# Seven block products for eight in the second feed-forward stage, with a new table of order

## The chip, the cores and the metric

The kernel runs on one core of a Trainium2 chip. Six queues matter here: TensorE (PE in the profile, PEld for its weight loads), VectorE (DVE), ScalarE (ACT), GpSimd (POOL), SyncE (SP, which issues most DMAs), and ScalarE's own DMA queue. The metric is device time in microseconds (us) of one execution; lower is better.

## The reference

Inputs are fp32. Attention over 2 batches, 8 heads, 768 positions and 64 dimensions is masked by equal hash buckets; two feed-forward stages follow it, on 1536 tokens of width 512:

```python
q_bits = (np.einsum('bhsd,dk->bhsk', q, proj) > 0)      # k likewise; proj is 64 x 6
mask = q_bucket[:, :, :, None] == k_bucket[:, :, None, :]
scores = np.where(mask, scale * q @ k.T, -1e9)
x = softmax(scores) @ v                                 # -> (1536, 512)
h = x @ w_in                                            # (512, 2048)
g = np.where(h >= 1, h, np.where(h <= -1, 0.0, (h + 1) ** 2 / 4))
y = g @ w_out                                           # first stage
return ((y @ w_a) * (y @ w_b)) @ w_out2                 # second stage, d_ff = 1536
```

The weights reach the device as 64-bit words, so each tile of them is rebuilt on chip from two 32-bit halves.

## The kernel before, in words

Every fp32 matrix product is done in three terms: an operand is split into a high part (a copy rounded to fp32r) and a low part (the operand less the high part), and high by high, high by low and low by high are added in PSUM. So each operand costs a copy (ScalarE or VectorE) and a subtraction (GpSimd or VectorE) besides the matmuls.

Tokens are worked in `NBLK` = 4 blocks of `TB` = 384. In the first stage (`kind` "in" and "out", `F1` = 16 slices) hidden slices of 128 are made from the 4 chunks of the width, and are added into 4 accumulators. In the second stage (`F2` = 12 slices) a slice f of block blk takes one contraction "a" and one "b" (`contract`, 12 matmuls each: 4 chunks x 3 terms, 384 columns), `t = a * b` (one copy out of PSUM, one product), a split of t into gh and gl, and "out2": 3 token tiles x 3 terms of 512 columns into `acc0` to `acc2`. Attention of the second batch runs beside the first blocks of the first stage.

The second stage's weights are made once: `conv_one` fetches a tile (`stage`, SP), joins its halves (one ScalarE and two VectorE instructions, into `wab`), and `keep` splits it into `wkh` and `wkl`, which stay in SBUF for all four blocks.

The order of the work on every engine is written out: `ORDER` is a table of 2,961 entries, and each entry names an engine and the next operation, as a step from the one before. Dependencies add the semaphores. Buffers come from pools with a set number of slots: `G` takes the space that attention leaves, `F` is the large one, `p` are two PSUM banks, `s0` one, `acc` four.

In PSUM and SBUF the names are `ap` and `bp` (contractions of the second stage), `hp` (of the first), `acc` (outputs), `xsh`/`xsl` (split activations), `y` (output of the first stage), `tk`, `tq`, `kp`, `kid`, `s` (attention's tiles), `plo` and `ptl` (low part of the probabilities, and its transpose by DMA).

At the start the projections `prj` come by two DMAs on SP, and six plus two dummy matmuls (`keep_busy`, tile `idle`) stand in a fixed place between attention's first transposes and its first `kp`.

Of the kernel before, what the change touches and what calls it, by code (L numbers as in the profile page):

```python
# [9 lines left out]
F32 = mybir.dt.float32  # L10
# [24 lines left out]
s s2 a4 v v-6 p10 v v p-5 s20 a-19 s23 s-28 v p11 p p a v-9 p10 s-17 v42 g a-17 v4 a-12 p3 a p-3 a s7 v p-5 a s7  # L35
v v p s-23 v p32 a v-10 a210 g v-200 v-7 p8 a p-12 v p19 p-4 s233 a v-237 a8 p2 s-1 a24 g a-45 v15 a s-4 v p33
s219 v-248 g9 a-4 a5 g13 v7 v p-20 v p-6 s335 a-324 p-2 a p-3 a v-7 a p24 v s-9 v208 v-198 p8 a a25 g a-43 p-6 v
a v211 g-193 a g8 p-12 v p6 a p v p7 v s-20 a s-11 a14 p19 a v-7 p4 a v-72 s285 p-197 v p-4 a-22 a19 p-4 v8 v4
v-11 v8 p6 v a170 v p-164 g-100 p67 s35 s-38 g16 a205 v g-253 g62 a6 a-22 v19 a31 a-35 v-62 v233 s-175 a s-26
p38 a p p26 v v v-27 s-9 s-1 g12 a p3 a p-14 a17 p-2 a v7 v-48 p36 a p23 a v s-13 g7 p14 v s-8 a-30 a18 g-49 g-1  # L40
a95 g p-52 v a s3 v-7 p9 v v160 p-141 v-4 a g8 p-12 a8 p11 a-20 v2 s188 p-180 v a10 a209 g s-217 p20 v-54 a55 v
p a v p-22 a-14 v13 p6 a p27 v p-33 v a-7 a179 p-138 a-22 v-1 v162 v s-141 a27 g p-53 v p14 v a11 s-14 a p40 a v
a-54 g16 v123 v-144 p38 s-47 p34 a14 g5 a-24 p20 a v-17 g10 a g-33 s138 g-92 v-47 p35 v p-6 v p28 a v s-40 p48 a
s141 p-167 v a187 v-267 s57 p49 v32 v a-72 v18 a90 v p-77 a8 a-26 a22 p19 v v-23 p54 a s-58 a p-12 v v s-5 p41 a
g-23 g9 s-27 p36 v s39 p-52 v a-8 s11 p28 a v36 p92 p-126 v v v-3 a-28 a-4 g22 a g16 p-20 v p-15 p31 v v44 g a55
v a-122 a144 v a-140 v21 p9 a v66 p-56 p-2 v a-23 a19 v82 g-121 g52 s-67 p40 p15 v g-3 p-3 p35 a-25 v-9 v57 a21
p-61 v18 s107 a v-125 s-32 g34 a-19 v22 v121 a-125 a14 p-4 v s-43 p37 v p15 a v-15 p16 v p7 a-19 g27 p15 s-52
v53 s-15 a-8 p p28 v-117 s59 g10 v113 a-85 v s14 s-29 p3 a-1 v7 g-10 s2 a-3 v12 s13 g-1 a13 p10 v-38 a70 a-69
g70 v-32 p-27 v a p41 v a-38 g18 a g6 p-10 v-71 p57 v-10 v25 a a11 v11 p-17 v p17 a p13 v a-31 a34 a-2 v-14 s-43
p30 v v p28 v p-17 a v p32 v s16 g-37 s-31 a69 a8 p-42 a v21 v13 v8 v-7 v-17 p-34 a a v s71 a g-88 g-25 v42 v72  # L50
a-59 p2 a a s-40 p57 a v-34 p41 a-4 g v-25 v59 a-44 a23 p-16 v s269 v-288 a g p23 p-2 v10 s-20 p17 v s66 a v
p-41 v-18 v60 a-41 s-45 a18 a11 p3 s23 a-22 v29 p-15 a p-25 v g10 v a-5 v p23 s-8 s-19 a-2 a38 p-55 v83 g-20 v21
p-50 a p21 v a-16 p10 v s-32 v8 p16 a4 a5 a13 g22 v-39 v-7 v8 p19 a a a-4 p-7 v a s34 v-24 p7 v p-35 p-2 p57 a32
s-68 s57 v-92 p66 a2 s-112 a116 v-33 p17 a5 v-1 v44 p22 a s-91 s104 p-67 a v-17 a p6 v5 g9 a-34 p19 v7 p-5 p31 v
a-4 p-18 v a-119 v137 a-10 v a-4 g-19 s-33 v72 p-15 g-41 p65 a61 a-94 v25 g18 s-41 a8 a p-6 a v12 v-6 a18 p-9 v
a-69 p111 a v-34 v-18 v p39 a-30 s13 v10 p25 v p-32 v a-4 v s-35 p31 a17 v18 g-17 p25 v-38 a15 a v p-21 a7 a28
# [24 lines left out]
a64 g p-74 v p6 v a-6 p32 v p-30 p14 a v-14 a27 g-23 g-42 p59 v v30 g p-38 g18 p4 a-14 v-7 a18 g12 v-69 p53 a8 a
s-13 v5 a p40 p-3 p-19 a v-11 a a-6 g p7 v a p28 v p-3 p-14 v s486 v-485 p11 p-16 v p7 v p36 a-50 a17 v-10 v-67
# [162 lines left out]
def attn_moe_kernel(ctx: ExitStack, tc: tile.TileContext, q, k, v, proj,  # L245
                    w_in, w_out, w_a, w_b, w_out2, consts, codes, out):
    nc = tc.nc
# [13 lines left out]
    WARM = 8  # L261
    NB1, NB2 = 6, 2
    RW = 3
    RL = 3
    AGAIN = "out", 5
    KEEP = 2
    NK = 27
# [945 lines left out]
```

## Time and profile before

| | |
|---|---|
| three runs before | 812.21 us median (811.88 to 812.91) |
| the profiled execution | 814.48 us, of which 812.6 us is the span from the first to the last instruction |
| PE busy | 783.4 us |
| DVE, ACT, POOL busy | 539.0, 414.1, 279.1 us |

How to read the profile: busy time of TensorE counts a matmul until its modelled end, so that consecutive matmuls overlap; the distance from one start to the next is what a matmul costs. For the other engines the time from one start to the next in a dense stretch is likewise a little less than the duration that a row gives.

### The profile page before, as it was taken

How to read it: one execution, taken by the hardware profiler on the slowest of the kernel's cores; microseconds unless marked ns; L12 is line 12 of the kernel's file. 1: busy time of each engine (PE TensorE's matmuls, PEld its weight loads, DVE VectorE, ACT ScalarE, POOL GpSimd, SP SyncE). 2: the span in 40 equal slices, each digit the busy share in tenths (PEclk: the TensorE clock that was granted, in tenths of full speed). 3: DMA queues.
4: the chain of work that ended last, by engine and by line, in shares of the span. 5: the costliest groups of instructions: out<-in, count | busy, mean ns of one | idle time of the engine just before them, and what ended most of it. 6: DMA issues, size and time to landing. Idle time of an engine off the chain costs nothing.

```text
span 812.6 us, 14548 instructions
## 1 busy us (share of the span) xinstructions
PE 783.4 (96%) x5716; PEld 728.2 (90%) x5716; DVE 539.0 (66%) x953; ACT 414.1 (51%) x732; POOL 279.1 (34%) x228
## 2 busy tenths in 40 slices
PE   7898799899999999999999999999999999999997
PEld 4677699899888999999999999999999999999997
DVE  5999799999998897989788788644322142133111
ACT  5998699798886876866454565312210111011101
POOL 1767444527564757652332310302100010011101
PEclk9999999999999999999999999999999999999999
DMA  6999999999978877750203454521010010001001
GB/s 187 201 220 206 207 230 261 217 175 248 219 131 166 171 139 133 120 110 1 78 29 107 150 156 129 156 78 52 4 37 1 0 40 1 1 1 40 0 1 40
DMA packets 197509, 90.28 MB, mean 111 GB/s; under 512 B 165056, under 2 KB 191936, under 8 KB 197440
## 3 DMA queue, kind: packets, MB, share of 16 engines
q1 hardware_dynamic: 197152, 89.15, 49.9%
q8 instruction: 45, 0.74, 0.4%
q10 hardware_dynamic: 288, 0.20, 0.1%
q14 instruction: 24, 0.20, 0.1%
HBM read 48.44 MB, written 3.15 MB: 63 GB/s over the span
## 4 chain that ended last, share of the span: by engine, by line
PE 79%; DVE 10%; DMA 5%; issue 2%; ACT 2%; POOL 1%; SPq 0%; DVEq 0%; POOLq 0%; ACTq 0%
PE hp L1021 14%; PE acc L1069 14%; PE ap L1021 12%; PE bp L1021 12%; PE acc L1105 12%; PE s L637 5%; PE pv L709 4%; DMA ptl<-plo 3%; DVE mn L640 2%; PE kp L541 1%; DVE plo L358 1%; DVE wlo L358 1%; PE kid L559 1%; DVE F L926 1%; PE tk L469 1%
## 5 line engine op out<-in xcount | busy, mean ns | idle before, releaser
L358 POOL TENSOR_TENSOR plo<-sm,phi 128x768 f16<-128x768 f32 x66 | 114.6, 1745 | 71.7 <-DVE phi L355 23.0
L358 POOL TENSOR_TENSOR gl<-t,gh 128x384 fp32r<-128x384 f32 x41 | 42.8, 1044 | 255.3 <-ACT gh L353 165.6
L1089 DVE TENSOR_TENSOR t<-t,bp 128x384 f32<-128x384 f32 x48 | 26.6, 553 | 121.6 <-PE bp L1021 121.6
L642 ACT ACTIVATE sm<-s,mn 128x768 f32<-128x768 f32 x96 | 86.2, 898 | 31.9 <-DVE mn L640 27.3
L640 DVE TENSOR_REDUCE mn<-s 128x1 f32<-128x768 f32 x96 | 91.2, 951 | 11.8 <-PE s L637 11.0
L353 ACT ACTIVATE gh<-t 128x384 fp32r<-128x384 f32 x62 | 32.4, 523 | 110.5 <-DVE t L1089 62.2
L353 ACT ACTIVATE t<-ap 128x384 f32<-128x384 f32 x27 | 13.2, 490 | 119.8 <-PE ap L1021 116.5
L1021 PE MATMUL ap<-xsh,wkl 128*128 128x384 f32 x192 | 64.5, 336 | 0.0
L358 POOL TENSOR_TENSOR wlo<-F,whi 128x512 fp32r<-128x512 f32 x35 | 48.9, 1403 | 45.2 <-ACT whi L353 19.3
L1021 PE MATMUL ap<-xsl,wkh 128*128 128x384 f32 x192 | 64.4, 336 | 0.0
L1021 PE MATMUL bp<-xsl,wkh 128*128 128x384 f32 x192 | 64.3, 335 | 0.0
L1021 PE MATMUL ap<-xsh,wkh 128*128 128x384 f32 x192 | 64.3, 335 | 0.0
L1021 PE MATMUL bp<-xsh,wkl 128*128 128x384 f32 x192 | 64.3, 335 | 0.0
L1021 PE MATMUL bp<-xsh,wkh 128*128 128x384 f32 x192 | 64.2, 334 | 0.0
L920 ACT ACTIVATE wab<-stage 128x512 f32<-128x512 f32 x71 | 47.1, 664 | 32.2 <-DVE wkl L358 8.9
L353 ACT ACTIVATE phi<-sm 128x768 f16<-128x768 f32 x71 | 59.2, 840 | 1.0
L637 PE MATMUL s<-kh,qt 128*128 128x384 f32 x192 | 55.4, 370 | 2.5 <-ACT sm L642 2.4
L1105 PE MATMUL acc<-wkh,gl 128*128 128x512 f32 x144 | 56.9, 395 | 0.0
L1105 PE MATMUL acc<-wkl,gh 128*128 128x512 f32 x144 | 56.7, 394 | 0.0
L1105 PE MATMUL acc<-wkh,gh 128*128 128x512 f32 x144 | 56.0, 389 | 0.0
L1043 ACT ACTIVATE t<-hp,half 128x384 f32<-128x384 f32 x64 | 36.8, 575 | 35.2 <-PE hp L1021 34.4
L1021 PE MATMUL hp<-xsh,whi 128*128 128x384 f32 x152 | 52.1, 343 | 0.1
(170 smaller groups left out, 2238.7 us busy)
## 6 DMA issues: line engine op xcount, KB each, us to landing
stage<-in_moe_w_out SPq DMA_DIRECT2D x31, 512.0 KB, 4.2
stage<-in_moe_w_in SPq DMA_DIRECT2D x16, 512.0 KB, 4.4
stage<-in_moe_w_a SPq DMA_DIRECT2D x12, 512.0 KB, 3.7
stage<-in_moe_w_b SPq DMA_DIRECT2D x12, 512.0 KB, 3.7
kn<-in_k SPq DMA_DIRECT2D x16, 192.0 KB, 3.8
out<-ob SPq DMA_DIRECT2D x12, 256.0 KB, 2.0
vn<-in_v SPq DMA_DIRECT2D x4, 384.0 KB, 4.8
vscan<-in_v SPq DMA_DIRECT2D x4, 384.0 KB, 5.0
```

What stands on the lines that cost most here:

```text
L353: nc.scalar.activation(dst, src, ACTF.Copy)
L358: (nc.vector if e == "dve" else nc.gpsimd).tensor_tensor(dst, a, b, ALU.subtract)
L637: nc.tensor.matmul(s()[:, i, 0:HC], x()[:, qs], t[i]()[:, 0:HC], start=(n == 0), stop=(n == 1))
L640: add({"dve": c_dve(S)}, lambda e: nc.vector.tensor_reduce(mn(), s()[:, :, 0:HC], AX.XY, ALU.min), r=[s], w=[mn])
L642: o = add({"act": c_act(S, True) + 0.093}, lambda e: nc.scalar.activation(sm().rearrange("p (c n) -> p c n", c=2), s()[:, :, 0:HC], ACTF.E ...
L709: nc.tensor.matmul(o[:, t, 0:D + 1 - i], w()[:, t, c, :], vcs[t]()[:, c, (1 - i) * D:(2 - i) * D + 1 - i], start=(n == 0), stop=(n == 3 * ...
L920: add({"act": 0.556}, lambda e: nc.scalar.activation(ab(), t()[:, :, :, 1].bitcast(F32), ACTF.Prelu, scale=SHIFT, alpha=SIGN), r=[t], w=[a ...
L1021: nc.tensor.matmul(o()[:, 0:TB], a()[:, kk, :], m(), start=(n == 0), stop=(n == 3 * KD - 1))
L1043: add({"act": 0.465}, lambda e: nc.scalar.activation(t(), o()[:, 0:TB], ACTF.Relu, bias=half, scale=0.5), r=[o], w=[t])
L1069: nc.tensor.matmul(ac()[:, 0:TB], a()[:, d, :], x(), start=(f == 0 and n == 0), stop=(f == F1 - 1 and n == 2))
L1089: add({"dve": c_dve(TB)}, lambda e: nc.vector.tensor_tensor(t(), t(), o()[:, 0:TB], ALU.mult), r=[o], w=[t])
L1105: nc.tensor.matmul(ac(), a()[:, ts], x().rearrange("p k n -> p (k n)"), start=(f == 0 and n == 0), stop=(f == F2 - 1 and n == 2))
```

## The change

The second stage takes two token blocks together. With a1, a2 and b1, b2 the two halves (over the width) of the a- and b-weights of a slice, and the activations of two blocks in halves b11, b21 (first block) and b12, b22 (second), the eight half-contractions are replaced by seven, on sums and differences of weights (s1 to s4) and of activations (t1 to t4). A half-contraction (`product`) is 2 chunks x 3 terms = 6 matmuls of 384 columns. Three PSUM banks X (`mx`), Y (`acc3`) and Z (`mz`) collect them, and `ca`, `cb`, `cc` in SBUF hold what is combined.

- `main` of the second stage: two passes sb, each with 12 slices "ab" and "ab2", the out2 of the first block between them, and then the 12 out2 of the second block from the kept products `cc`.
- Weights: hi and lo parts aren't kept any more. For each slice and pass `weights` forms four sums (128 x 256, tile `ws`), splits three pairs of 512 columns (`wkh`, `wkl`) and one of 256 (`wkb`). The joined words stay in `G` for the first `KA` = 7 slices; those of the other 5 are fetched and joined again for the second pass. `osplit` splits w_out2 for each block anew.
- Activations: `tsplit` forms eight differences (`td`) and ten splits (`tph`, `tpl`) beside the usual split of one block, at the end of the first stage and again during the out2 of block 1.
- The projections' two DMAs go on ScalarE's queue; the dummy matmuls are ordered only before the first score tile; GpSimd may take the high part of the probabilities; and the whole table `ORDER` is another one (3,520 entries), for attention and the first stage too.

```diff
-zb = Buf("z", None, None)
+zb, zz = Buf("z", None, None), Buf("z", None, None, "zz")
 def projections():
-        add({"sp": DMA["tiny"]}, get, w=[(zb, 0)])
...
+        for i in range(2):
+            nc.scalar.dma_start(out=prj[i * D:(i + 1) * D], in_=proj)
...
-        add({"act": c_act(S), "dve": c_dve(S, True)}, lambda e: copy_on(e, hi()[:, jj, :], sm()),
+        add({"act": c_act(S), "dve": c_dve(S, True), "pool": 0.1 + S * 1.55e-3}, ...
...
-    for blk in range(NBLK):
-        ab = [[("a", blk, f), ("b", blk, f)] for f in range(F2)]
-        main += ab[0]
+    n1 = len(main)
+    for sb in range(NBLK // 2):
         for f in range(F2):
-            if f + 1 < F2:
-                main += ab[f + 1]
-            main.append(("out2", blk, f))
+            main.append(("ab", sb, f))
+            if f:
+                main.append(("out2", 2 * sb, f - 1))
+            main.append(("ab2", sb, f))
+        main.append(("out2", 2 * sb, F2 - 1))
+        main += [("out2", 2 * sb + 1, f) for f in range(F2)]
...
+    lasts[max(i for i in range(n1) if main[i][0] == "in")] = "ab", 0
+    lasts[main.index(("out2", 1, F2 // 4))] = "ab", 1
...
+    def pair(src, view, hi, lo, n):
+        add({"act": c_act(n), "dve": c_dve(n, True)}, lambda e: copy_on(e, hi(), view()), r=src, w=[hi.buf])
+        add({"pool": c_pool(n), "dve": c_dve(n)}, lambda e: sub_on(e, lo(), view(), hi()), ...)
...
+    def weights(sb, f):
+        wa, wb = (w32[f, k] if f < KA else w32.pop((f, k)) for k in "ab")
...
+        # s1 = b1 + b2, s3 = a1 - b1, s2 = s1 - a1, s4 = a2 - s2
+            add({"pool": c_pool(h), "dve": c_dve(h)}, lambda e, ...: add_on(e, d(), x(), y(), op), ...)
...
+    def ab(i, sb, f):
+        mop[i] = product(X, X, u[0], 0, "b11", p, True, [s1])
+        product(Y, Y, u[0], 1, "b21", p, True)
+        snap(s1, X, X)
+        plus(s1, Y, Y, ALU.add)
+        product(X, X, u[2], 1, "t2", p, False, [s2])
+        product(Z, zv, u[2], 0, "t1", p, True)
+        snap(s2, X, X)
+        product(X, X, u[3], 0, "t3", p, False, [s3])
+        snap(s3, X, X)
+        plus(s3, Z, zv, ALU.add)
+
+    def ab2(sb, f):
+        product(X, X, u[1], 0, "t4", p, False)
+        product(Z, zv, u[3], 1, "b22", p, False)
+        plus(s1, X, X, ALU.mult)
+        gt[2 * sb, f] = split(s1)
+        plus(s2, Z, zv, ALU.add)
+        add({"pool": c_pool(TB), "dve": c_dve(TB)}, ... s3 = s3 * s2 ...)
+        gt[2 * sb + 1, f] = s3
```

On TensorE at the very start of the program, before: six key transposes (`tk`), then dummy matmuls, then the query transposes (`tq`), more dummies, and the first hash product `kp`.

```order
L469 MATMUL tk<-cst,kn 128x128 x6
L454 LDWEIGHTS warm
L454 MATMUL idle<-warm 128x512
...
L509 MATMUL tq<-eye,qsh 128x128 x3
...
L541 MATMUL kp<-qt,zq_h 103x384
```

The same place after the change:

```order
L529 MATMUL tq<-eye,qsh 128x128 x3
L489 MATMUL tk<-cst,kn 128x128 x6
L474 LDWEIGHTS warm
L474 MATMUL idle<-warm 128x512
...
L562 MATMUL kp<-qt,zq_h 103x384
L562 MATMUL kp<-qt,zq_l 103x384
```

The query transposes moved ahead of the key transposes and of the six dummies, two of which now stand behind `kp`'s six matmuls.

On TensorE in the second stage, before, one contraction and the output term behind it (block 0; chunks xsh0 to xsh3 with their low parts):

```order
L1021 MATMUL ap_7967<-xsh0_7785,wkh_7110 128x384
L1021 MATMUL ap_7967<-xsl0_7787,wkh_7110 128x384
L1021 MATMUL ap_7967<-xsh0_7785,wkl_7139 128x384
L1021 MATMUL ap_7967<-xsh1_7791,wkh_7110 128x384
L1021 MATMUL ap_7967<-xsl1_7793,wkh_7110 128x384
L1021 MATMUL ap_7967<-xsh1_7791,wkl_7139 128x384
L1021 MATMUL ap_7967<-xsh2_7773,wkh_7110 128x384
L1021 MATMUL ap_7967<-xsl2_7775,wkh_7110 128x384
L1021 MATMUL ap_7967<-xsh2_7773,wkl_7139 128x384
```

After, in the first pass, two products with an output term between them:

```order
L1162 MATMUL mx_8362<-xsh0_7709,wkh_7471 128x384
L1162 MATMUL mx_8362<-xsl0_7798,wkh_7471 128x384
L1162 MATMUL mx_8362<-xsh0_7709,wkl_8016 128x384
L1162 MATMUL mx_8362<-xsh1_7745,wkh_7471 128x384
L1162 MATMUL mx_8362<-xsl1_7751,wkh_7471 128x384
L1162 MATMUL mx_8362<-xsh1_7745,wkl_8016 128x384
L1267 MATMUL acc2_7983<-whi_8065,gh_8305 128x512
L1267 MATMUL acc2_7983<-wlo_8340,gh_8305 128x512
L1267 MATMUL acc2_7983<-whi_8065,gl_8307 128x512
L1162 MATMUL mz_8309<-tph_7238,wkh_8096 128x384
L1162 MATMUL mz_8309<-tpl_7558,wkh_8096 128x384
L1162 MATMUL mz_8309<-tph_7238,wkl_8099 128x384
```

Groups of twelve became groups of six in the same shape, and the banks change at each group.

On VectorE in the second stage, before, a stretch of block 1, when all weights stand ready (t: the slice's product, gl: its low part):

```order
L1089 TENSOR_TENSOR t_8512<-t_8512,bp_8531 128x384
L355 COPY t_8546<-ap_8545 128x384
L358 TENSOR_TENSOR gl_8571<-t_8512,gh_8560 128x384
L355 COPY t_8584<-ap_8583 128x384
L1089 TENSOR_TENSOR t_8584<-t_8584,bp_8597 128x384
L358 TENSOR_TENSOR gl_8627<-t_8584,gh_8625 128x384
```

After, a stretch of the first pass (L928 and L931 join words, L376 are low parts, L1172 reads a PSUM bank, L1066 forms a sum of weights):

```order
L1172 TENSOR_TENSOR cb_8286<-cb_8286,mz_8309 128x384
L931 SCALAR_TENSOR_TENSOR F_8353<-stage_8351,F_8353 128x512
L373 CAST whi_8440<-F_8353 128x512
L1172 TENSOR_TENSOR ca_8259<-ca_8259,mx_8258 128x384
L1066 TENSOR_TENSOR ws_8400<-wab_8324,wab_8395 128x256
L376 TENSOR_TENSOR gl_8446<-ca_8259,gh_8444 128x384
L373 COPY cc_8432<-mx_8362 128x384
L1172 TENSOR_TENSOR cc_8432<-cc_8432,mz_8451 128x384
L928 TENSOR_SCALAR wab_8470<-wab_8470 128x512
L1172 TENSOR_TENSOR ca_8363<-ca_8363,acc3_8408 128x384
L931 SCALAR_TENSOR_TENSOR wab_8470<-stage_8468,wab_8470 128x512
L1172 TENSOR_TENSOR ca_8363<-ca_8363,mx_8362 128x384
```

VectorE got the reads of three banks, the joining of words, sums of weights and low parts of weights into one stretch; these instructions that free a PSUM bank (L1172) stand behind weight work in one queue.

## Rows read from the trace of the kernel before

**Rows 1.** Page: busy time of each engine, and the span in 40 slices.

```profile
PE 783.4 (96%) x5716; PEld 728.2 (90%) x5716; DVE 539.0 (66%) x953; ACT 414.1 (51%) x732; POOL 279.1 (34%) x228
PE   7898799899999999999999999999999999999997
DVE  5999799999998897989788788644322142133111
```

**Rows 2.** Page: chain that ended last, by engine and by line.

```profile
PE 79%; DVE 10%; DMA 5%; issue 2%; ACT 2%; POOL 1%; SPq 0%; DVEq 0%; POOLq 0%; ACTq 0%
PE hp L1021 14%; PE acc L1069 14%; PE ap L1021 12%; PE bp L1021 12%; PE acc L1105 12%; PE s L637 5%; PE pv L709 4%; DMA ptl<-plo 3%; DVE mn L640 2%; PE kp L541 1%; DVE plo L358 1%; DVE wlo L358 1%; PE kid L559 1%; DVE F L926 1%; PE tk L469 1%
```

**Rows 3.** Four stretches: length; busy us of PE, PEld, DVE, ACT, POOL; clock; DMA.

```profile
0.00:100.00 100.00, 80.50 (x759) 63.27 (x760) 83.52 (x156) 76.52 (x130) 54.95 (x50) 0.95 1.02 203
100.00:375.00 275.00, 269.49 (x2605) 250.93 (x2604) 250.17 (x420) 222.07 (x385) 153.01 (x117) 0.99 0.86 173
375.00:500.00 125.00, 125.00 (x727) 124.64 (x726) 102.84 (x187) 67.65 (x126) 33.92 (x28) 1.00 0.33 102
506.00:808.40 302.40, 302.36 (x1596) 283.36 (x1595) 96.94 (x181) 43.74 (x86) 37.17 (x33) 1.00 0.09 28
```

**Rows 4.** Chain in order of time, second stage: start, us, what, matmuls.

```profile
599.19 4.16 PE bp L1021 x24
649.99 7.52 PE acc L1105 x33
```

**Rows 5.** Groups of instructions: count, busy us, mean ns, idle before and its cause.

```profile
L1021 PE MATMUL ap<-xsh,wkh 128*128 128x384 f32 x192 | 64.3, 335 | 0.0
L358 POOL TENSOR_TENSOR wlo<-F,whi 128x512 fp32r<-128x512 f32 x35 | 48.9, 1403 | 45.2 <-ACT whi L353 19.3 <-DVE whi L355 8.9 <-DVE F L926 6.7
L358 POOL TENSOR_TENSOR gl<-t,gh 128x384 fp32r<-128x384 f32 x41 | 42.8, 1044 | 255.3 <-ACT gh L353 165.6 <-DVE gh L355 87.5 <-issue 1.8
```

**Rows 6.** Timeline of the start: start us, duration, instruction, idle before.

```profile
5.50 0.36 ACT L353 ACTIVATE qsh<-qnh 128x192 fp32r<-128x192 f32 x1 [3.27 <-DMA qnh<-in_q]
7.56 2.77 PE L454 MATMUL idle<-warm 128*128 128x512 bf16 x6
8.98 0.17 DVE L343 CAST p_h<-prj 128x6 fp32r<-128x6 f32 x1 [0.66 <-DMA prj<-in_proj]
9.76 0.95 PE L509 MATMUL tq<-eye,qsh 128*128 128x128 f32 x3
10.75 0.49 ACT L520 ACTIVATE qt<-tq 128x384 fp32r<-128x384 f32 x1 [2.46 <-PE tq L509]
11.29 0.42 PE L541 MATMUL kp<-qt,zq_h 128*103 128x384 f32 x1
```

**Rows 7.** Timeline of DVE and POOL in the first stage, 406 to 413 us.

```profile
406.95 0.56 DVE L1052 SCALAR_TENSOR_TENSOR t<-t,hp 128x384 f32<-128x384 f32 x1 [1.62 <-ACT t L1048]
...
407.84 0.68 DVE L358 TENSOR_TENSOR wkl<-F,wkh 128x512 fp32r<-128x512 f32 x1
408.44 0.41 DVE L355 CAST wkh<-F 128x512 fp32r<-128x512 f32 x1
408.78 0.55 DVE L358 TENSOR_TENSOR gl<-t,gh 128x384 fp32r<-128x384 f32 x1
409.25 1.78 DVE L358 TENSOR_TENSOR wlo<-F,whi 128x512 fp32r<-128x512 f32 x1
410.96 1.31 DVE L358 TENSOR_TENSOR wkl<-wab,wkh 128x512 fp32r<-128x512 f32 x1
412.19 0.68 DVE L358 TENSOR_TENSOR wkl<-F,wkh 128x512 fp32r<-128x512 f32 x1
...
406.33 1.30 POOL L358 TENSOR_TENSOR wkl<-F,wkh 128x512 fp32r<-128x512 f32 x1
408.94 1.54 POOL L358 TENSOR_TENSOR wkl<-F,wkh 128x512 fp32r<-128x512 f32 x1 [1.30 <-DVE wkh L355]
410.45 1.27 POOL L1050 TENSOR_TENSOR t<-t 128x384 f32<-128x384 f32 x1
```

More of the change, by code (lines that the diff above doesn't have):

```diff
@@ L40 @@
[L40 to L44, printed above, removed]
@@ L263, in attn_moe_kernel @@
     RW = 3
-    RL = 3
+    KA = 7
     AGAIN = "out", 5
@@ L512, in tq @@
         first = (b, h, c) == (0, 0, 0)
-        o = add({"pe": 0.42}, mm, r=[(qs, 0), (qs, 1)], w=[s, qt],
-                after=[keep_busy(NB1, busy["o"])] if first else ())
         if first:
-            busy["k"] = keep_busy(NB2, o)
+            keep_busy(NB1, busy["o"])
+        o = add({"pe": 0.42}, mm, r=[(qs, 0), (qs, 1)], w=[s, qt])
+        if first:
+            keep_busy(NB2, o)
         def scaled(e):
@@ L544, in signs @@
         add({"pe": (0.181 if b else 0.19) * n}, mm, r=[(zb, 1)] + qs + ks,
-            w=[s, bit], after=[busy["k"]] if (b, h) == (0, 0) and early else ())
+            w=[s, bit])
         add({"act": c_act(HC, True) + 0.093}, lambda e: nc.scalar.activation(
@@ L928, in conv_one @@
             r=[t], w=[r])
-        fw[n] = r
-        if moe2:
-            keep(n, th, tr)
+    def conv_one(n):
+        kind, f, _ = corder[n]
+        here = n in again
+        fw[n] = Buf(place[n][0], [128, KD, 128], F32)
+        words(kind, f, fw[n], here, far=far[-1:] if not here and n >= sizes["F"] - 4 * KF else ())
     def w_split(n):
-        n = min(n, len(main))
+        n = min(n, n1)
         w_conv(n - 1 - LMIN)
@@ L1024, in contract @@
                    w=[o, *more], after=after)
-    firsts = [i for i, o in enumerate(main) if o[2] == 0 and o[0] in ("in", "a")]
+    firsts = [i for i, o in enumerate(main) if o[0] == "in" and o[2] == 0]
     lasts = {}
@@ new lines, in attn_moe_kernel @@
+    emit2 = []
+    at_f = {(k, sb, f): i for i, (k, sb, f) in enumerate(main[n1:], n1)}
+    for f in range(F2):
+        u = at_f["ab", 0, f]
+        for n, x in enumerate("ab"):
+            emit2.append((4 * F1 + 6 + 3 * (2 * f + n) if f < KA else u - 7 + n, "word", 0, f, x))
+        emit2.append((u - 4, "set", 0, f, None))
+        emit2.append((u - 3, "word", 0, f, "out2"))
+        u = at_f["ab", 1, f]
+        if f >= KA:
+            emit2 += [(u - 7 + n, "word", 1, f, x) for n, x in enumerate("ab")]
+        emit2.append((u - 4, "set", 1, f, None))
+        for blk in range(NBLK):
+            emit2.append((at_f["out2", blk, f] - 2, "osplit", blk, f, None))
@@ new lines, in product, with mm @@
+    def product(bank, view, w, c, x, p, start, more=()):
+        wh, wl = w
+        ps = [p[x, k] for k in range(2)]
+        h = DM // 2
+        def mm(e):
+            n = 0
+            for k in range(2):
+                sl = slice(c * h + k * 128, c * h + (k + 1) * 128)
+                for a, m in ((wh, ps[k][0]), (wh, ps[k][1]), (wl, ps[k][0])):
+                    nc.tensor.matmul(view()[:, 0:TB], a()[:, sl], m(), start=(start and n == 0), stop=(n == 5),
+                                     skip_group_check=not start)
+                    n += 1
+        return add({"pe": 1.045}, mm, r=[wh.buf, wl.buf] + [y.buf for q in ps for y in q], w=[bank, *more])
@@ L1139, in attn_moe_kernel @@
         w_split(i + 3)
+        while emit2 and emit2[0][0] <= i:
+            _, what, n, f, x = emit2.pop(0)
+            if what == "word":
+                word(n, f, x, i)
+            else:
+                (weights if what == "set" else osplit)(n, f)
         run_op(i)
```

379 lines of the change are left out of this document (237 added, 142 removed).

## The prediction

> **What bounds the kernel now.** First the page, for the busy time of each engine by slice: TensorE is busy 96% of the span, and every slice from the seventeenth on has the digit 9, while VectorE falls from 7 to 9 in the first slices to 1 to 4 in the last ten [rows 1]. Then the chain of waits: 79% of it is TensorE, and the second stage's lines, `ap`, `bp` and `acc` L1105, hold 12% each [rows 2]. Then the stretches, because the share of the whole is a mean over stages with different limits [rows 3]. In 0 to 100 us TensorE is idle for 19.5 us, and VectorE and ScalarE set the pace. In 100 to 375 us TensorE is idle for 5.5. From there it has no gap. The second stage (506 to 808.4 us) is TensorE alone: VectorE is at 97 of 302 us, ScalarE at 44, GpSimd at 37, and the granted clock is 1.00, the 2.4 GHz level. So what leaves TensorE's list in the second stage comes off the time, unless the other engines then become late.
>
> **What a matmul costs.** A row gives 335 ns for one [rows 5], but they overlap. The chain gives the distance: 24 contraction matmuls took 4.16 us, 0.173 each, and 33 of the output's 7.52, 0.228 each [rows 4]. Check: 1,152 x 0.173 + 432 x 0.228 = 298 us, against 302.4 for the stage [rows 3], or 1.5% more by the clock than by my prices.
>
> **The change, part by part.**
>
> Removed: for each of 12 slices and 2 passes, 48 contraction matmuls become 42. That is 144 x 0.173 = 24.9, with the stage's 1.5% 25.3; I take **-25.1 us**. The shape of each matmul and of its weight load stays. The output terms stay: 432.
>
> Added to the other engines, hidden only while they keep up. I count the first pass (from its first product to its last), in which TensorE has 110 us of work. Prices are distances in a dense stretch [rows 7]: a subtraction of 512 columns takes VectorE 0.60 us (407.84 to 408.44), a copy of 512 0.34, a subtraction of 384 0.47. I take the shifts that join words at the same prices as copy and subtraction, reads of PSUM at 0.47, and a sum of 256 columns at 0.34, as an estimate from the step between 384 and 512. VectorE's list there has 56 reads of PSUM and 33 subtractions of 384 (41.8 us), 32 subtractions and 21 joins of 512 (31.8), 28 copies or shifts of 512 (9.5), 21 pieces of 256 (7.1) and 3 copies (0.8): **91 us, 82% of TensorE's 110**. Before, VectorE ran at 82% in 375 to 500 us, waits for GpSimd included, with no gap on TensorE [rows 3]. ScalarE's list is 117 instructions, mostly at 0.5 to 0.6, some 65 us, and doesn't bind.
>
> GpSimd's list in the pass is 8 of 512 at 1.40, 5 of 384 at 1.04 [rows 5], and 31 of 256 at 0.68 (estimate, same step): 37.5 us. That matters for VectorE: at 409.25 a subtraction of 512 took 1.78 us, and ended 0.55 after GpSimd's instruction from 408.94 had ended; the next took 1.31 beside GpSimd's from 410.45 [rows 7]. The two together needed 2.94 where two free ones need 1.20. GpSimd's three instructions in those rows last 4.11 us and cost VectorE 1.74, 42%. So VectorE's 91 become 91 + 0.42 x 37.5 = **107 us, 97% of TensorE's time**. The bounds are 91 (nothing lost) and 128.5 (all of it lost).
>
> At 97% in-order queues don't mesh: with VectorE at 91% in 100 to 375 us TensorE was idle for 2% of the time [rows 3]. What waits is seen in the queue that stands in the section on the change: the reads that free banks X, Y and Z stand behind joins and weight parts, and TensorE's next product into the bank waits for them. I take 3 to 4% of the pass, 3.8 us. In the second pass VectorE has 88 us of work, GpSimd 54 and TensorE 127, so 88 + 0.42 x 54 = 111, 87%: 0.5 us.
>
> At the hand-over from the first stage, a dozen differences and low parts and eleven copies stand between the first difference (`td`) and the first product, while TensorE has about 7 us of the first stage's work left. VectorE's 14 instructions there take 14 x 0.47 = 6.6 us. It fits barely; I take 0.7 us of gap, between 0 and 5. Together these are **+5 us**, with 0 and +18 as ends without the worst case below.
>
> Ten more weight tiles are fetched in the second pass. The DMA engines are at 9% in that stage [rows 3], so nothing; without that cover each would cost some 4 us once. Weights split again rather than kept are in the lists above.
>
> The start: `kp` at 11.29 follows ScalarE's `qt`, which ended at 11.24, which follows `tq`, which stood behind six dummies (7.56 to 9.69) though its input began to be split at 5.50 [rows 6]. With `tq` ahead of `tk`, `qt` is ready long before; then the dummies, and VectorE's list (two key copies and low parts, the projections' split of six instructions, which took from 8.98 to 9.83), set `kp` at about 9.8. So 1.5 us earlier. The projections landed just before 8.98, issued on SP at fifth and sixth place; on ScalarE's queue they are second and third. If the gain is lost behind the next wait it is 0; at most it is 2.2, the length of the dummies. **-1.5 us**.
>
> The rest of the table: attention and the first stage have the same work in another order. Up to the second stage's first matmul VectorE has 741 instructions for 774 (among them 8 fewer high parts, 4 fewer low parts of the probabilities, 3 fewer scans), ScalarE 651 for 645, GpSimd 216 for 198. In 0 to 100 us VectorE is busy for 83.5 and ScalarE for 76.5 [rows 3], so work taken from VectorE can shorten a stretch of which TensorE idles a fifth. But GpSimd's added 18 instructions block VectorE's as above, and the transposes of the low parts (`ptl`, 3% of the chain [rows 2]) don't get shorter. Ends: -7 (all of VectorE's relief of some 11 us less what GpSimd takes) and +5 (a queue order that meshes worse by a quarter of the 19.5 us of gaps). I take **-1.5 us**.
>
> The sum: -25.1 + 5 - 1.5 - 1.5 = -23.1 on the profiled execution's 814.48 (a span of 812.6 and 1.9 around it): 791.4. That execution stands 2.3 above the median of the three runs, 812.21, from which I subtract the same: 789.1. I say **789 us**.
>
> **The rivals.**
>
> *VectorE and GpSimd take turns in full* (ends on the other side). If no subtraction, join, fast copy or sum on VectorE runs beside any GpSimd instruction, and reads of PSUM don't fill in, then the first pass needs 91 + 37.5 = 128.5 us against 110, and the second 88 + 54 = 142 against 127: +33.5 in place of +4.3, that is 789 + 29 = 818 us, slower than before. It decides from the point at which 94% of GpSimd's time is lost to VectorE (where the loss is 28 us). For it: the two subtractions above, which lost 1.74 of 2.81 us. Against it: the third GpSimd instruction (406.33 to 407.63), which cost nearly nothing, since VectorE was reading PSUM from 406.95 on, and the 125 us from 375 on, where VectorE had 102.8 us busy and GpSimd 33.9, 137 together, and TensorE saw no gap [rows 3]. The Trainium skill has this as a rule: "SBUF — State Buffer", section "SBUF: two separate sides", says the port pair that VectorE shares with GpSimd is an exclusive lock, held for a whole instruction, for VectorE's two-input and fast modes. By that rule alone the sum would be this rival's; the rows agree on the blocking, and show that a third to a half of it falls beside reads of PSUM and idle time. Chance 0.04.
>
> *VectorE becomes the bound of the first pass*, between the two: half to all of the lost time is not taken back, and the hand-over costs 5 us. Then the first pass takes 115 to 122 us, and the time is 794 to 803 us. For it: 97% is an estimate from three GpSimd instructions, and VectorE reached 91 to 95% at best in the trace. Chance 0.20.
>
> *The other order of attention gives more than the products*: -7 there and little loss in the passes: 779 to 782 us. For it: 33 fewer instructions on VectorE, in the stretch where VectorE is the slowest. Against: ScalarE is nearly as full. Chance 0.10.
>
> *The change doesn't save what the count says*: groups of six that change banks could run at a worse distance than groups of twelve. But output terms of three matmuls in a row already change banks between contractions at no cost in the stage's sum above. A loss of a tenth of the gain, 2.5 us, lies inside the forecast's range. Beyond it 0.01, at 805 to 812.
>
> **How the numbers follow.** The forecast, 782 to 794, has 0.65, and its value is the prediction. With the rival above it to 799 and the one below it from 779, the range 779 to 799 holds somewhat over 0.8. A difference under 0.2%, 1.6 us, couldn't be told from none. Faster: 0.95; the same: 0.01; slower: 0.04, the first rival.
>
> **What the profile will show.** Right: the second stage in about 281 us for 302, TensorE's count down by 144, VectorE at 90% or more in the first 110 us of that stage and under 85% in the last 130, gaps on TensorE there of 3 to 6 us in total that end with VectorE's reads of `mx`, `acc3` or `mz`; the first `kp` near 9.8 us; the first product of the second stage at 502 to 506 us. Wrong: a second stage of 290 us or more with VectorE waiting on GpSimd (subtractions over 1.2 us in numbers), a first product after 508, or a first product before 498, which would say that the table of attention was worth more than the products' loss.

## The result, and the profile after

| | before | after |
|---|---|---|
| median, four runs each | 812.56 us (811.88 to 813.42) | 782.58 us (781.57 to 782.83) |
| profiled execution, its span | 814.48, 812.6 us | 782.61, 780.8 us |

The ratio is 0.9628, with a 95% interval of 0.9611 to 0.9645: 30.0 us less, where 23.1 were forecast. The prediction of 789 is 6.4 us too high; the time lies inside the forecast's 782 to 794, 0.6 us above its lower end.

The page of the changed kernel, its busy times and two of its rows by slice, answers to [rows 1]:

```profile
PE 755.5 (97%) x5572; PEld 699.6 (90%) x5572; DVE 655.3 (84%) x1179; ACT 496.8 (64%) x901; POOL 365.4 (47%) x315
PE   7887899999999999999999999999999999999998
DVE  6998899999988868986876778899989989888765
```

TensorE has 144 matmuls fewer, 5,572 for 5,716. VectorE, which stood at 1 to 4 tenths at the end, is now at 8 or 9 until the last three slices. The chain of waits, beside [rows 2], is TensorE's for 83%, and VectorE's part fell from 10% to 7%:

```profile
PE 83%; DVE 7%; ACT 3%; DMA 3%; issue 2%; POOL 2%; SPq 0%; ACTq 0%; DVEq 0%; POOLq 0%
```

The stretches, beside [rows 3] (length; busy us of PE, PEld, DVE, ACT, POOL with counts; granted clock; DMA). The second stage runs from its first product, at 497.80, to 777.1; 635.6 is the middle of its 1,440 matmuls:

```profile
0.00:100.00 100.00, 82.81 (x803) 65.14 (x804) 84.59 (x159) 85.31 (x145) 56.45 (x53) 0.98 1.00 214
100.00:375.00 275.00, 273.39 (x2628) 256.31 (x2625) 239.01 (x415) 224.93 (x393) 162.98 (x126) 1.00 0.82 169
497.80:635.60 137.80, 136.51 (x720) 127.61 (x720) 128.00 (x239) 72.08 (x144) 48.54 (x48) 1.00 0.25 79
635.60:777.10 141.50, 140.05 (x723) 128.74 (x721) 109.54 (x202) 53.10 (x104) 59.84 (x54) 1.00 0.16 50
```

VectorE is busy for 93% of the first half and 77% of the second. TensorE's idle time fell from 19.5 to 17.2 us in the first 100, and from 5.5 to 1.6 up to 375.

All of TensorE's waits in the second stage, from the view of waits (us in all, times, the longest):

```profile
PE mz L1162 <- DVE cc L1172: 1.4, 1, 1.4
PE mx L1162 <- ACT ca L371: 0.6, 1, 0.6
PE mz L1162 <- DVE tpl L376: 0.5, 1, 0.5
PE acc L1162 <- DVE xsl L376: 0.2, 1, 0.2
```

The last three fall within 9 us of the first product, the first one at 690. Between them nothing waits.

So the two traces divide the time thus. The kernel before still had 12 first-stage matmuls behind its first contraction at 505.83, 2.1 us of work, so its front ends at 507.9, and its second stage of 1,584 matmuls takes 300.5 us to 808.4. After, the front ends at 497.8, the stage takes 279.3. **Front: -10.1. Second stage: -21.2. End: -0.5.** Together -31.8, the difference of the spans. Forecast were -3 and -20.1. The gain that was not foreseen is in front of the change's main part.

### The profile page after: what moved, and what is told of

Same layout as the page of the kernel before. It is cut to its first block, busy times and chain, and to the rows that moved or that the text cites. A ratio compares the mean times of both kernels' runs of the same rounds, so it can differ in the third digit from the quotient of the medians.

```text
span 780.8 us, 14758 instructions
## 1 busy us (share of the span) xinstructions
PE 755.5 (97%) x5572; PEld 699.6 (90%) x5572; DVE 655.3 (84%) x1179; ACT 496.8 (64%) x901; POOL 365.4 (47%) x315
## 4 chain that ended last, share of the span: by engine, by line
PE 83%; DVE 7%; ACT 3%; DMA 3%; issue 2%; POOL 2%; SPq 0%; ACTq 0%; DVEq 0%; POOLq 0%
PE hp L1029 17%; PE acc L1241 15%; PE acc L1267 13%; PE mx L1162 12%; PE s L658 6%; PE mz L1162 6%; PE pv L731 5%; PE acc L1162 3%; PE kp L562 2%; DMA pth<-phi 2%; DVE mn L662 1%; DMA kn<-in_k 1%; ACT sm L664 1%; PE tk L489 1%; PE kid L580 1%
## 5 line engine op out<-in xcount | busy, mean ns | idle before, releaser
L376 POOL TENSOR_TENSOR plo<-sm,phi 128x768 f16<-128x768 f32 x70 | 121.6, 1744 | 59.9 <-ACT phi L371 33.3
L664 ACT ACTIVATE sm<-s,mn 128x768 f32<-128x768 f32 x96 | 86.1, 897 | 24.3 <-DVE mn L662 20.5
L376 POOL TENSOR_TENSOR wlo<-F,whi 128x512 fp32r<-128x512 f32 x38 | 52.0, 1374 | 42.1 <-ACT whi L371 27.8
L1267 PE MATMUL acc<-whi,gl 128*128 128x512 f32 x144 | 56.7, 394 | 0.0
L1267 PE MATMUL acc<-wlo,gh 128*128 128x512 f32 x144 | 56.6, 393 | 0.0
L1267 PE MATMUL acc<-whi,gh 128*128 128x512 f32 x144 | 56.1, 390 | 0.0
L1241 PE MATMUL acc<-gh,whi 128*128 128x384 f32 x144 | 51.7, 359 | 0.0
L731 PE MATMUL pv<-vc,pth 128*128 128x65 f16 (+1 forms) x1152 | 51.0, 194 | 0.2 <-DVE xsl L376 0.2
L1029 PE MATMUL hp<-xsh,wlo 128*128 128x384 f32 x152 | 51.1, 336 | 0.0
L1029 PE MATMUL hp<-xsl,whi 128*128 128x384 f32 x152 | 51.0, 336 | 0.0
L658 PE MATMUL s<-kl,q 128*128 128x384 f32 x192 | 49.8, 340 | 0.4
L1241 PE MATMUL acc<-gh,wlo 128*128 128x384 f32 x144 | 48.5, 337 | 0.0
L1241 PE MATMUL acc<-gl,whi 128*128 128x384 f32 x144 | 48.4, 336 | 0.0
```

The lines of the kernel that those rows point to most:

```text
L376: (nc.vector if e == "dve" else nc.gpsimd).tensor_tensor(dst, a, b, ALU.subtract)
L658: nc.tensor.matmul(s()[:, i, 0:HC], x()[:, qs], t[i]()[:, 0:HC], start=(n == 0), stop=(n == 1))
L664: o = add({"act": c_act(S, True) + 0.093}, lambda e: nc.scalar.activation(sm().rearrange("p (c n) -> p c n", c=2), s()[:, :, 0:HC], ACTF.E ...
L731: nc.tensor.matmul(o[:, t, 0:D + 1 - i], w()[:, t, c, :], vcs[t]()[:, c, (1 - i) * D:(2 - i) * D + 1 - i], start=(n == 0), stop=(n == 3 * ...
L1029: nc.tensor.matmul(o()[:, 0:TB], a()[:, kk, :], m(), start=(n == 0), stop=(n == 3 * KD - 1))
L1241: nc.tensor.matmul(ac()[:, 0:TB], a()[:, d, :], x(), start=(f == 0 and n == 0), stop=(f == F1 - 1 and n == 2))
```

## The experiments

**The two halves, apart.** The order of attention and of the first 70 first-stage steps was taken from one kernel, all that follows from the other. Of the table, that is the first line and those that follow (the changed kernel with the old order in front):

```diff
-s3 v3 v p10 s-16 v a17 s9 a p-18 a p-4 v v s22 a v-28 s301 p-290 v-3 p7 s-16 v41 g p-28 a3 p5 v p-5 v a284 v
+s v4 s-2 a3 v v-5 p9 p5 v-4 v p-5 s20 a-19 s23 p-15 p a v-9 p10 s-16 v41 g a-17 v4 a-12 p3 a p-3 a s7 v p-5 a s7 v v p
...
```

> The changed kernel's second stage behind the order that the kernel before had for attention and the first 70 of the first stage's 128 steps; everything else, the projections' queue too, as in the changed kernel. What the traces say of the front: the first product came 8.0 us earlier (497.81 for 505.83), 10.1 when the 12 first-stage matmuls that the kernel before still had behind it are counted. Theory 1, the order in front is worth these 10 us: 792 to 794 us, the first product at 506 to 509, and the long waits of the kernel before are back (ptl some 3 us near 82, kp some 3 us near 157), with the granted clock at 0.5 behind them. Theory 2, the front of that one trace was luck, or the projections' queue alone: 783 to 786, the first product at 498 to 501. Under both the second stage itself takes 279 to 281 us.

Measured: 792.27 us (790.86 to 792.59), ratio to the kernel before 0.9751 (0.9731 to 0.9771); the first product at 507.8, the stage 279.0 us long.

The reverse, the kernel before with the changed kernel's start, order and engines in front:

```diff
-s s2 a4 v v-6 p10 v v p-5 s20 a-19 s23 s-28 v p11 p p a v-9 p10 s-17 v42 g a-17 v4 a-12 p3 a p-3 a s7 v p-5 a s7
+s3 v3 v p10 s-16 v a17 s9 a p-18 a p-4 v v s22 a v-28 s301 p-290 v-3 p7 s-16 v41 g p-28 a3 p5 v p-5 v a284 v s-294 a
...
```

> The other half: the kernel before, with its eight half-contractions, its weights kept and its order from step 70 of the first stage on, behind the changed kernel's order for attention and the start. Theory 1 (the order in front is worth 10 us, whatever stands behind it): 802 to 804 us, first contraction of the second stage near 496. Theory 2 (luck, or worth something only with the new second stage): 810 to 813. Together with the run above, the two parts should add up to the whole, 30 us.

Measured: 803.10 us (802.82 to 803.22), ratio 0.9889 (0.9874 to 0.9903). So the front is worth 9.7 us by the one and 9.4 by the other, and the second stage the other 20.5: theory 1, and the parts add up. One part of the first expectation failed: with the old front the 3 us wait for `ptl` near 82 did not come back (1.4 us in three waits in all). That wait differs from one execution to the next: two later traces with the same order in front have it with 1.8 us at 84 and 2.1 at 83.

**Where the front loses.** In the run with the old front, a timeline of VectorE, GpSimd and TensorE from 153 us on (start, duration, instruction, idle before):

```profile
153.50 1.58 DVE L369 TENSOR_TENSOR plo<-sm,phi 128x768 f16<-128x768 f32 x1
...
154.23 1.98 POOL L369 TENSOR_TENSOR wlo<-F,whi 128x512 fp32r<-128x512 f32 x1
...
155.00 1.75 DVE L924 SCALAR_TENSOR_TENSOR F<-stage,F 128x512 int32<-128x512 int32 x1
156.68 0.94 DVE L655 TENSOR_REDUCE mn<-s 128x1 f32<-128x768 f32 x1
...
157.55 0.54 DVE L536 TENSOR_SCALAR qt<-tq 128x384 fp32r<-128x384 f32 x1
...
158.14 0.65 PE L555 MATMUL kp<-qt,zq_h 128*103 128x384 f32 x1 [2.82 <-DVE qt L536]
```

VectorE's join (L924, 0.69 us when free) took 1.75 beside GpSimd's `wlo`, and `qt`, whose PSUM input was ready, stood behind it and behind the minimum `mn`. TensorE waited 2.82 us, and the windows show what went with it (same columns as above; the clock is the third figure from the end):

```profile
155.00:157.10 2.10, 0.33 (x2) 0.00 (x1) 2.10 (x3) 0.00 (x0) 1.21 (x1) 1.00 1.06 257
157.10:163.90 6.80, 5.76 (x26) 5.24 (x27) 5.35 (x9) 5.79 (x11) 1.55 (x2) 0.50 0.75 169
```

The clock fell at 157.1, while TensorE still waited, and was at 0.50, the 1.2 GHz level, for 6.8 us. So the join was moved behind the three instructions that it held up, and `qt` also went ahead of `mn`:

```diff
-L924 SCALAR_TENSOR_TENSOR F<-stage,F
-L655 TENSOR_REDUCE mn<-s
 L536 TENSOR_SCALAR qt<-tq
+L655 TENSOR_REDUCE mn<-s
 L1217 SCALAR_TENSOR_TENSOR t<-t,hp
+L924 SCALAR_TENSOR_TENSOR F<-stage,F
```

> The kernel with the old order in front (792.3 us), with one change on VectorE near 155 us: the joining of a word, which there took 1.75 us for 0.69 beside a GpSimd instruction, goes behind the scaling of qt, the row minimum mn and the reading of hp, which stood behind it. In that kernel TensorE waited there 2.8 us for qt, and the granted clock was at 0.5 from 157.1 to 163.9. Theory 1, this one place is worth most of what the order between 100 and 165 us lost (4.2 us by the traces): 788 to 789.5, the wait under 1 us and no stretch at 0.5 near 157. Theory 2, the wait moves to the next bank or to the word that is now late: 791.5 to 792.5.

Measured: 789.99 us (788.10 to 791.28), ratio 0.9722 (0.9698 to 0.9745), where the old front has 0.9751: 2.3 us less by the medians. The same ten microseconds in both runs, the old front's and the one with the join moved:

```profile
155.00:165.00 10.00, 7.18 (x57) 6.35 (x57) 7.45 (x11) 6.49 (x12) 3.50 (x3) 0.66 0.75 173
```

```profile
155.00:165.00 10.00, 8.45 (x88) 7.42 (x87) 9.14 (x16) 7.89 (x15) 3.83 (x3) 1.00 0.91 211
```

The wait shrank to 0.28 and 1.27 us came back at the next bank (`s`, for `sm`), as theory 2 has it, but the clock stayed at 1.00 and 88 matmuls were started for 57. The two medians are each uncertain by more than half a microsecond, so the traces carry this: the first product came at 505.2 for 507.8. What the join and the swap of `qt` with `mn` gave, each by itself, was not tried.

A second run was to part the wait from the clock:

```diff
+            if fill:
+                for i in range(14):
+                    nc.tensor.matmul(s()[:, 0:HC], warm.to_broadcast([128, 128]), warm.to_broadcast([128, HC]),
+                                     start=True, stop=True)
```

> The kernel with the old order in front, with 14 dummy matmuls of 384 columns on TensorE ahead of the kp that waits at 155 us, in its own bank, which kp then overwrites. The wait for qt stays (2.8 us, of which the dummies fill some 2.5). Theory 1, TensorE's waiting is what takes the clock down, and the stretch at 0.5 behind it costs 1.4 us of its own (4.2 less the 2.8 of waiting): 790.5 to 791.3, the clock at 1.00 from 155 to 165. Theory 2, the clock falls there anyway: 792 to 793.

Measured: 795.21 us (794.91 to 796.01), and it settles nothing: the operation's wait for `qt` stood ahead of the dummies, so that they began at 158.32, after it, and took 3.8 us, with the clock at 0.50 until 161.7. How the loss at this place divides into wait and clock stays open.

**The start.** Keys ahead of queries on SP again, the query transposes behind the dummies:

```diff
-L529 MATMUL tq<-eye,qsh 128x128 x3
 L489 MATMUL tk<-cst,kn 128x128 x6
 L474 MATMUL idle<-warm 128x512
+L529 MATMUL tq<-eye,qsh 128x128 x3
```

> The changed kernel with three places of the start as the kernel before had them: the keys issued ahead of the queries on SP, the query transposes on TensorE behind the key transposes and the six dummies, two dummies behind them, and qt on ScalarE behind the key copy and two scans. The projections stay on ScalarE's queue. Theory 1, the earlier start (the first score tile at 12.80 us for 15.83) is worth its 3 us at the end: +2 to +3.5, 784.6 to 786, the first score tile at 15 to 16. Theory 2, the queues of VectorE and ScalarE catch up within attention: 0 to +1.

Measured: 783.20 us (782.09 to 783.81), 0.6 above the changed kernel, with the first score tile at 14.8 us for 12.8. Theory 2: of 2 us lost at the start, at most 1 is left at the end.

**The price of the products.**

```diff
                 for a, m in ((wh, ps[k][0]), (wh, ps[k][1]), (wl, ps[k][0])):
+                    if x == "b22":
+                        nc.tensor.matmul(view()[:, 0:TB], a()[:, sl], m(), start=False, stop=False,
+                                         skip_group_check=True)
```

> The changed kernel with one product of the seven (the one on b22) issued twice, so that the second stage has 1,152 contraction matmuls again and its output holds that product twice. Nothing is added on the other engines. Theory 1, TensorE alone sets the second stage: 144 x 0.173 and 1.5% more, +25 us, 807 to 809. Theory 2, VectorE sets the first pass and hides the product there: half of it, +12 to +14, 795 to 797. The stage's waits (3.5 us) would shrink a little under both.

Measured: 805.00 us (804.57 to 805.37), +22.4. That is theory 1 less 2.7 us: the wait of 1.4 us at 690 is gone there, and the stage takes 302.9 us for 279.3:

```profile
497.00:799.90 302.90, 301.51 (x1585) 281.50 (x1584) 233.12 (x441) 125.16 (x248) 106.35 (x102) 1.00 0.19 60
```

**How much room VectorE has.** The joining instruction done twice for the words of the first pass:

```diff
+        def join(e):
+            for _ in range(times):
+                nc.vector.scalar_tensor_tensor(
```

> The changed kernel with VectorE's joining instruction (L931) done twice for the 21 or 22 words of the first pass: 12.6 to 13.2 us more work for VectorE there, the same result. VectorE was busy for 103.5 of 112 us in the first pass and TensorE had 110.7 us of work. Theory 1, VectorE has its 8% of room and no more: VectorE's list comes to 116 to 117, so the pass gets 5 to 7 us longer, 787 to 790. Theory 2, VectorE is at its edge already (97% as forecast): +11 to +13, 794 to 796. Theory 3, part of its busy time is waiting for GpSimd, which shrinks when it is later: 0 to +2, 782.6 to 785.

Measured: 793.56 us (793.38 to 795.22), +11.0. Theory 2. The stage's first half, and TensorE's two largest waits there:

```profile
497.10:646.40 149.30, 140.75 (x721) 126.24 (x720) 143.62 (x261) 71.63 (x144) 49.11 (x48) 1.00 0.23 73
```

```profile
PE mz L1165 <- DVE cb L1175: 2.6, 3, 1.1
PE mx L1165 <- ACT cb L371: 1.6, 2, 1.2
```

VectorE was busy for 15.6 us more, the half grew by 11.5, and VectorE's share came to 96% for 93%. So the joins, 12 to 13 us by the list and 15.6 by busy time, found 2 to 4 us of room, not 8. What VectorE does not use there it mostly spends waiting for TensorE's products (4.3 us of the first 112 in the changed kernel) and ScalarE's copies (2.5).

**GpSimd beside VectorE.** GpSimd's instructions twice:

```diff
+        for _ in range(2 if e == "pool" and op is not ALU.mult else 1):
+            (nc.vector if e == "dve" else nc.gpsimd).tensor_tensor(dst, a, b, op)
```

> The changed kernel with GpSimd's sums, differences and low parts of the second stage done twice each (all but its products of two tiles), with the same result: some 36 us more for GpSimd in the first pass, 78 of 112 us in all, and some 50 us in the second, 116 of 165. VectorE's instructions are the same. Theory 1, VectorE's instructions on SBUF wait while GpSimd's run, at 30% of GpSimd's time (the first pass: VectorE 103.7 us busy, 91 by its list at free prices, GpSimd 42.4): VectorE loses 11 us more in the first pass, of which the run with the joins done twice says that only 1 to 2 are free: +8 to +11, 791 to 794, and VectorE's subtractions of 512 columns get longer on average than the 0.69 to 0.80 us of the changed kernel. Theory 2, the long instructions on VectorE have another cause: GpSimd still has room, 0 to +2, up to 785.

Measured: 841.52 us (840.55 to 842.79), +58.9. Both theories are far off in time. The two halves of the stage, one group of VectorE's instructions (765 ns in the changed kernel; the two larger groups of this shape grew less, from 748 to 805 and from 694 to 820), and the largest waits of TensorE:

```profile
500.80:664.60 163.80, 143.90 (x721) 127.74 (x720) 145.40 (x237) 71.66 (x144) 94.11 (x92) 0.99 0.21 66
664.60:835.40 170.80, 150.00 (x723) 132.80 (x721) 126.69 (x204) 53.28 (x104) 107.38 (x96) 0.96 0.13 42
```

```profile
L376 DVE TENSOR_TENSOR wlo<-F,whi 128x512 fp32r<-128x512 f32 x15 | 14.9, 998 | 0.1
```

```profile
PE acc L1272 <- POOL wlo L376: 8.8, 3, 5.1
PE mz L1167 <- DVE cc L1177: 5.4, 3, 3.2
PE mx L1167 <- POOL wkb L376: 4.9, 2, 3.2
```

On VectorE theory 1 holds: with 45.6 us more for GpSimd in the first half VectorE was busy 17.4 us longer at the same list (38%), and in the second 17.2 for 47.5 (36%). But the time went further than that. The stage is 55.3 us longer: 38.0 us of it is idle time of TensorE, and 17.3 is busy time for the same matmuls, with the granted clock at 0.99 and 0.96. Of all its waits there, 40.7 us, 17.6 end with results of GpSimd, `wlo` and `wkb` first, and 16.5 with results of VectorE, which in the second half is at 74%.

All of GpSimd's instructions of these kinds given to VectorE, in their places:

```diff
-L376 POOL TENSOR_TENSOR wkl<-ws,wkh 128x512
+L370 DVE TENSOR_TENSOR wkl<-ws,wkh 128x512
...
```

> The changed kernel with all 107 instructions of GpSimd on the second stage's weights, activations and products given to VectorE, in the same places of the order; GpSimd is idle there but for 7 low parts. VectorE's list grows by some 17.7 us at free prices in the first pass and some 27 in the second. Theory 1, VectorE gets back what it lost to GpSimd (12.7 us in the first pass): its list comes to 109 us for 103.7, +4 to +6, and 0 to +2 in the second pass: 787 to 790. Theory 2, nothing comes back: 121 us, +11 to +14, 794 to 797. Theory 3, without the losses the queue meshes better and the time is the same within 1 us.

Measured: 817.14 us (813.87 to 818.24), +34.6, above every theory, and slower than the kernel before (ratio 1.0052, 1.0030 to 1.0073). The two halves of the stage and TensorE's largest waits:

```profile
497.00:650.00 153.00, 142.66 (x721) 127.72 (x720) 136.39 (x286) 71.71 (x144) 2.04 (x2) 0.99 0.22 71
650.00:808.40 158.40, 145.24 (x722) 130.50 (x721) 120.19 (x249) 53.10 (x104) 6.22 (x6) 0.98 0.14 45
```

```profile
PE acc L1261 <- DVE wlo L370: 6.2, 5, 3.2
PE mx L1156 <- DVE wkb L370: 5.3, 3, 2.7
PE mx L1156 <- ACT cb L365: 5.2, 4, 1.8
```

The profiled execution, 813.87 us, is the fastest of the eight. VectorE's list went most of the way to theory 1: 107 instructions worth 45 us by the list made it 19 us longer, so that some 26 us came back for 100 us less of GpSimd. But it is at 89% and 76%, and still TensorE waits: weight parts that stood on a second queue now stand in line with the reads of banks. The table of order was made for two queues. The Trainium skill, "Perfetto Trace Analysis", section "Optimizing Scalar/DVE Operations", warns that moving work between GpSimd and VectorE might not help, since they share a port. Here the lists bear that out in part, and the time does not: in this order, without GpSimd, the kernel is slower by 34.6 us.

**The wait at 690.** The changed kernel there, VectorE, GpSimd and TensorE:

```profile
689.45 1.46 POOL L376 TENSOR_TENSOR wkl<-ws,wkh 128x512 fp32r<-128x512 f32 x1 [0.43 <-POOL ws L1066]
...
689.69 1.63 DVE L1066 TENSOR_TENSOR cc<-cc,cb 128x384 f32<-128x384 f32 x1
...
690.87 1.58 POOL L376 TENSOR_TENSOR wkl<-wab,wkh 128x512 fp32r<-128x512 f32 x1
691.24 0.54 DVE L1172 TENSOR_TENSOR cc<-cc,mz 128x384 f32<-128x384 f32 x1
...
691.84 0.44 PE L1162 MATMUL mz<-tph,wkh 128*128 128x384 f32 x1 [1.45 <-DVE cc L1172]
```

It is [rows 7] again: 0.55 us of work took 1.63 beside GpSimd, and the read that frees bank Z stood behind it. That read itself took 0.54 us with GpSimd busy throughout, and none of the stage's 96 reads of this kind (L1172) took over 0.56. Two pairs were swapped:

```diff
-L1066 TENSOR_TENSOR td<-y,td
 L376 TENSOR_TENSOR tpl<-td,tph
+L1066 TENSOR_TENSOR td<-y,td
...
-L1066 TENSOR_TENSOR cc<-cc,cb
 L1172 TENSOR_TENSOR cc<-cc,mz
+L1066 TENSOR_TENSOR cc<-cc,cb
```

> The changed kernel with two pairs swapped in VectorE's order: the read of mz into cc goes ahead of the product cc x cb behind which TensorE waited for 1.45 us at 690, and at the hand-over one low part (tpl) goes ahead of one difference (td). Theory 1, TensorE's waits in the second stage go to the end one for one: -1.5 to -2, 780.6 to 781.1. Theory 2, the wait comes back at the next bank: 0 to -0.5. It may be too small to tell apart.

Measured: 780.20 us (779.70 to 781.64), 2.4 below. Because the times overlapped, it was run again beside the changed kernel:

> The changed kernel with the two swaps on VectorE again, now beside the changed kernel itself on the same chip: 1.5 to 2.5 us below it if TensorE's waits in the second stage go to the end one for one, 0 to 0.5 if not.

> The changed kernel itself, as the base for the run with two swaps: 782 to 783.

Measured: 782.15 us (780.40 to 782.32) and 782.44 (781.85 to 783.66). In the traces of that pair the stage takes 277.8 us for 279.4, and the wait at 690 is gone: there the waits go to the end one for one, which is theory 1. By the medians it is 0.3 in this pair, which the expectation gave to the other theory, and 2.4 across the two runs before; the median of all eight executions is 781.1 for 782.6. It is the best version found, by 1 to 2 us, if it is better at all.

## Why the prediction was right in sum, and where it was not

**The products, -25.1: right.** Issued again, 144 matmuls cost 22.4 us, 23.6 in the stage, and 25.0 there with the 1.4 us of waiting that they hid. TensorE sets the second stage.

**VectorE's lag, +5: right in sum, wrong in place.** By the stage's length the loss is 25.1 - 21.2 = 3.9 us, by the named waits 2.7; without these the stage is 276.6 us, 23.9 less than before, so that the other 1.2 is the size of the products. But 3.8 were forecast for the first pass, and behind its first 9 us that shows none; the hand-over has 1.3 for 0.7, the second pass 1.4 for 0.5. VectorE was at 92% of the first 112 us, not 97%:

```profile
497.80:609.80 112.00, 110.71 (x598) 105.14 (x598) 103.53 (x194) 58.07 (x115) 42.38 (x43) 1.00 0.29 90
```

That is less of a miss than it looks: the joins found 2 to 4 us of room, so the rival in which VectorE becomes the bound was close. The step "at 97% in-order queues don't mesh" failed: VectorE was all but full, and the order put no read of a bank late in the first pass. Of the gaps of 3 to 6 us that were to end with VectorE's reads of banks, 2.7 came, and 1.4 of them end so.

**What GpSimd costs VectorE: 42% of GpSimd's time forecast, 26 to 38% measured.** The doubled instructions say 36 to 38%, the first pass 30% (103.5 us busy for a list of 91, GpSimd 42.4), and the run without GpSimd 26%. The rival of full turns is out: its point was 94%. (What falls free is by the prediction's own rows 38 to 58%, rather than its "a third to a half".) The Trainium skill's rule ("SBUF — State Buffer", "SBUF: two separate sides"; an exclusive lock for a whole instruction) fits each blocked row (1.75 for 0.69, 1.63 for 0.55), and the reads of PSUM, at 0.54 us beside GpSimd, are one reason why the whole costs about a third.

**The start, -1.5: at most 1 is left at the end**, though the first `kp` came at 8.01 us, not 9.8. Beside [rows 6], the timeline of the start shows why it came so early:

```profile
4.00 1.06 PE L529 MATMUL tq<-eye,qsh 128*128 128x128 f32 x3
...
4.98 0.36 DVE L373 COPY kn<-kn 128x384 f32<-128x384 f32 x1 [1.04 <-DMA kn<-in_k]
...
6.16 1.47 PE L474 MATMUL idle<-warm 128*128 128x512 bf16 x6
...
7.42 0.16 DVE L361 CAST p_h<-prj 128x6 fp32r<-128x6 f32 x1
...
8.01 0.39 PE L562 MATMUL kp<-qt,zq_h 128*103 128x384 f32 x1 [0.38 <-DVE zq_l L364]
```

The queries, now first on SP, let `tq` run at 4.00 for 9.76, and the six dummies, which all stand ahead of `kp` (two more stand behind it), took 1.47 us for 2.77, with the clock there at its full level and not at 0.50. What `kp` waited for last is VectorE's list, as forecast, but that list ran earlier: the copy of the keys at 4.98 for 6.17, and the split of the projections from 7.42 for 8.98.

**The rest of the table, -1.5, bounds -7 and +5: the step that failed.** The front is worth 9.4 to 9.7 us, some 9 without the start, beyond my bound. I bounded an order by how much work it takes off VectorE, and the prediction's own mark, "a first product before 498", was met at 497.8. Counted by the columns that TensorE had streamed (dummies left out; the total is the same in both), the trace with the old front stood some 2 us behind the changed kernel's at 150 us, 7.0 at 200 and 10.5 from 400 on; with the join moved, some 2, 4.1 and 7.4. So about half of the loss fell near 157, where one blocked join (and the minimum behind it) held `qt` back and TensorE's clock fell during the wait; 2.3 us came back by putting these few instructions into another order. Some 2 us more went in the 110 us behind it: TensorE is busy for 107.1 of them with the old front (165 to 275 us), and for 109.3 with the new (155 to 265). Two waits make up most of that. The changed kernel has neither, and both stayed when the join was moved (1.04 and 1.25 us there):

```profile
214.24 0.55 PE L482 MATMUL tk<-cst,kn 128*128 128x128 f32 x3 [1.12 <-DVE t L1217]
...
246.98 0.61 PE L651 MATMUL s<-kh,qt 128*128 128x384 f32 x2 [1.35 <-ACT sm L657]
```

What these two are worth at the end was not tried, nor were the order and the choice of engines, which the same table makes, tried apart. Of the rivals the one with the chance of 0.10, attention's order, came nearest: the front gave its 7 us and more, while the passes lost what the forecast said. Its reason, fewer instructions on VectorE, is not what the moved join shows, since that took no work away; how far it holds for the rest is open. That the time still lies within the forecast, with this term past its own bound, is luck.

## What to carry to other kernels

When a change brings a new order for everything, look for the long single waits that it can remove, with the clock behind them, and not only at the work that it takes off an engine: here one such place held about half of what the old front lost. Swapping one half of the order at a time shows what each is worth. A busy share is no measure of room: at 92% VectorE could take 2 to 4 us more, and at 76%, with GpSimd's work in its queue, it made TensorE wait. An instruction that GpSimd can block belongs behind the reads of PSUM in VectorE's queue where TensorE waits for these, since they were not blocked here.

## What the runs showed of the hardware

With the old front TensorE waited for 2.82 us up to 158.14; its granted clock fell to 0.50 at 157.1, within the wait, and stayed there for 6.8 us. After waits of 0.28 and 1.27 us at the same place it stayed at 1.00. Such falls differ between executions: in the changed kernel's trace the clock was at 0.50 from 70.4 to 73.8 with no single wait of TensorE over 1.2 us in the ten before, and in a second trace of the same kernel it was at 1.00 there.

Fourteen dummy matmuls inside the operation that waited did not fill its wait: they began when it had ended, at 158.32.

Beside GpSimd, instructions of VectorE that read and write SBUF took up to 1.75 us for 0.69 and 1.63 for 0.55; reads of PSUM stayed at 0.54 to 0.56 us.
